# A new issue order for a retention-plus-GELU kernel: one table of 955 words replaced by another

## The chip, the cores and the metric

The kernel runs on one core of one Trainium2 chip. The metric is the time of one execution in microseconds of device time. The engines are named as in the profile: PE (TensorE matmuls), PEld (TensorE weight loads), DVE (VectorE), ACT (ScalarE), POOL (GpSimd) and SP (SyncE, which here only issues DMAs).

## The reference

The first half is a retention layer (a recurrent attention with a decay per head), the second a two-layer network with a tanh GELU. q, k and v are float32 of shape (4, 8, 768, 64), w_in is 512 x 2048, w_out is 2048 x 512, and the result is 3072 x 512.

```python
gamma = 1.0 - 2.0 ** (-5.0 - np.arange(H))
for t in range(S):
    state = gamma * state + einsum('bhd,bhe->bhde', k[:, :, t], v[:, :, t])
    y[:, :, t] = D ** -0.5 * einsum('bhd,bhde->bhe', q[:, :, t], state)
x = y.transpose(0, 2, 1, 3).reshape(B * S, H * D)
h = x @ w_in
g = 0.5 * h * (1 + tanh(sqrt(2 / pi) * (h + 0.044715 * h ** 3)))
out = g @ w_out
```

## The kernel before, in words

**Tiling.** The 768 steps are cut into six chunks c = 0 to 5 of 128 steps. In each chunk and each of the four batches b the retention is three kinds of product: A = k q^T within the chunk, masked by the decay; y = A v plus q times the state carried in; and the state's update. A chunk then gives 512 rows of x, which go through w_in, GELU and w_out. Chunks 0 and 1 do the first layer by plain products (`m1_raw`), chunk 0 the second too (`m2_raw`). Chunks 2 to 5 (first layer) and 1 to 5 (second) use a scheme of seven products on half-size blocks (`m1_w`, `m2_w`), which needs sums of blocks: `xs` from x, `u_w` from w_in, `t_w` from w_out, `s_g` from the GELU's output. All these sums are recorded on one helper line, L447.

**Items and the table.** The work behind the lead-in is recorded as 954 items by `op` and `pe`: each has a number, a kind, the values it needs and gives, and the buffers that it takes and frees. The table `ORDER` names every item once by a letter for the engine (p PE, v DVE, a ACT, g POOL, s SP) and its number. The loop at L1268 emits the items in that order, so the table fixes the order in each engine's queue, the engine of those items that may run on more than one, and which PSUM bank or buffer an item takes (the one that has been free longest, by place in the table). A word like w3 emits three filler matmuls (L193). Each engine works through its queue in order and waits at the first instruction whose inputs aren't there.

**What the numbers stand for** where the prediction names them:

- p168 to p188: retention of chunk 0 (transposes L269, A L291, y L322, state L333). p190 to p236: first layer of chunk 0 (L422), p805 to p826 its second layer (L568). p239 to p274: retention of chunk 1 (transposes L280, A L291, state in L310, y L322, state L333). p276 to p306: first layer of chunk 1. p325 to p360, p451 to p480, p571 to p600, p691 to p716: retention of chunks 2 to 5. p365 to p431, p485 to p551, p605 to p671, p721 to p787: their first layer (L545, 4 matmuls each). p829 to p951: second layer of chunks 1 to 5 (L557, 8 matmuls each).
- L217, L219: copies and casts on ACT, POOL or DVE. L234: scaling by a decay (q, k or v). L342: evA, the masked copy of A out of PSUM. L349: evY, the scaled copy of y to x. L354: evS, four instructions that update the state. L438: GELU. L447: adds out of PSUM (`add`) and all block sums. L704: the transposes of q on DVE (`trq`).
- g0 to g5: POOL's triggers of the last six weight loads (L403, L412); the first two are issued in the lead-in. g6 is the `hold` (L776), a one-element copy that needs the third w_out chunk; all later loads of rows stand behind it.
- s11 to s118: SP's loads of q, k and v, each of 256 KB (L787); q of chunks 3, 4 and 5 comes as one item of 16 DMAs each, s60, s85 and s110 (L730, `loadq`). Stores of results (L578) are in the same queue. The casts of these q blocks are `castq` and `cast2`.

Of the kernel before, what the change touches and what calls it, by code (L numbers as in the profile page):

```python
# [13 lines left out]


ORDER = """
v8 v9 g0 g1 g10 g2 g3 g4 g5 p168 a167 w3 p173 p171 v170 a7 v169 p178 a172 w2 p188 a187 p180
p176 v174 v175 p184 p182 a183 p190 a181 a189 p192 v135 p186 v177 v179 v136 v143 v159 p206
p194 v144 v147 g6 a185 p196 s11 s12 s13 s14 s15 a191 g25 s16 g28 a193 s17 a195 s18 s19 s20
p222 p208 p210 p224 a223 p226 a225 p228 s21 g31 s22 g34 v139 v151 p230 p232 p198 a227 p200  # L20
a209 a205 a197 a229 p212 a231 p234 a221 a211 a199 p236 p202 p214 p216 p805 p218 a201 v146
v160 a233 v23 v163 v164 p204 v138 a213 a215 p806 a207 p220 p807 v155 p808 p809 p810 p811 v24
a203 a219 a217 p812 p813 p814 p817 a815 s35 s36 v26 v152 s37 v162 v140 v27 a818 s38 s39 s40
p239 v237 v238 p245 a244 a235 p820 v243 v141 v156 p242 v240 v241 p248 v247 v246 v29 p261
p823 v142 s41 p824 p825 p264 v263 p266 a265 p826 p276 p278 a827 v148 a275 p280 v158 v32 v33
p257 a277 v30 p251 s42 a279 s43 s44 p282 p284 v154 g54 g55 a821 v165 a249 a255 v256 p260
v250 p254 p262 a281 s45 s46 s47 v258 s816 p286 v253 v252 a283 s822 p288 a287 p268 a267 p272
g48 a49 g51 g52 v259 p270 v166 v269 p274 a57 g58 v273 v149 p290 p292 p294 p296 a291 a293
v271 p298 p300 a289 v137 p302 v307 s60 p304 p325 s61 v150 v308 v310 s62 v157 a295 a297 v311
g312 p343 g53 g56 v309 a285 v145 a299 a301 v50 s63 s819 p337 v323 v324 s64 s65 a335 v342  # L30
a303 g59 p306 v336 v341 a305 p331 g321 a330 g319 g320 a329 v315 p340 v339 v338 g322 p328
v327 p829 p830 v316 a831 p346 v344 g313 p334 g69 v326 v332 v333 p832 v345 p833 p348 p347
p350 p354 p358 v349 p352 p356 v355 p360 p835 p836 v351 p367 a73 a837 v357 v353 p384 p365 v70
g361 g363 a77 a75 p382 v359 a366 a383 v368 g79 v834 s66 s67 s828 s68 p838 p839 p372 p389
p399 p387 v385 a81 g83 g362 g314 v317 p401 p370 a369 g71 s85 s86 s87 g364 a400 a386 v153
v402 a388 a373 p404 a371 v74 v78 g76 a390 p841 p406 p377 v82 p374 v378 a405 a403 a407 a379
p391 g84 v375 a376 v392 v318 a393 p408 v409 p416 a417 s88 p380 a381 p411 a840 s89 g72 s90
g80 p397 a398 p394 v395 a396 p842 v412 a413 v843 v433 v437 v435 v161 p423 a424 p414 p421
p418 v419 v434 a422 g94 p844 p845 a410 a415 g441 v846 s847 g443 g438 g442 p428 p425 v426
g440 a420 v429 p451 a450 p460 a449 v459 s91 a96 a430 p848 v458 s92 p431 a432 p457 v455 v456  # L40
p454 v452 a427 g445 p463 p849 a850 g97 v462 v453 p852 p853 v461 p466 p467 v464 v465 p468
a854 p472 p480 v479 p474 p470 p478 v469 s851 v471 v477 g446 p476 v473 v475 a106 a102 s93 g98
g100 p855 p856 v857 p858 p502 a503 g439 g104 a108 g481 g483 p859 g484 g482 g109 v103 v107
s110 s111 g444 v95 s112 p485 s113 a486 s114 p861 p571 v569 v448 p580 a579 a860 a570 g105
g119 g101 p862 g121 p507 p492 p504 a508 a578 v505 p490 a493 p487 v488 a491 v447 p509 a510
p519 v436 p494 p497 a489 a506 p514 p511 v498 a499 v495 a496 a520 p864 v515 p521 a863 a516
v512 a513 p500 s115 a501 p536 p865 g553 s116 s117 p517 p543 a537 a518 v866 v99 g554 g557
g558 v522 p867 a544 p524 a525 p526 a527 a523 p868 v869 s870 g556 p528 g126 v529 p538 p541
a542 p531 v532 a533 p534 a530 a535 p871 p545 v539 a540 p872 a873 s874 s118 v546 a547 p548
v561 g562 v549 a550 p551 g130 p577 a552 g565 g567 g566 p586 v584 v585 p574 p875 p876 a877  # L50
p878 p879 v575 p583 v573 v572 p588 g563 v576 g560 v581 v582 p587 p590 p592 p598 v589 v591
p596 v595 a127 p594 v593 g601 v555 p600 v599 v564 v559 g603 v880 p881 p882 p884 p605 a883
p885 p639 p622 p607 p624 g604 a123 a606 a623 a125 a886 v597 g131 g133 v625 v608 p612 a626
a613 v120 v128 a640 p887 v132 p888 p610 a609 p617 p641 p644 g602 a611 v618 v642 a645 p627
a628 p614 p629 v615 a619 g122 a630 p648 p656 g568 a657 p631 p620 a616 v889 a621 v632 p646
a647 p634 p637 a638 v124 v635 a636 v673 p658 v674 v659 a633 a660 p890 g134 g677 g678 p691
a643 v649 v689 p661 a662 v690 p891 v892 p663 p651 p665 a129 a664 g680 v652 v666 p654 a650
a655 a653 g681 g682 p700 a699 a698 p697 v695 v696 p668 v669 p671 s893 a672 a667 a670 p898
v675 v687 p894 p895 g685 p694 v693 p703 g686 p706 v705 v692 p899 g679 p901 p902 a900 v903
p904 a896 s897 v701 v702 v704 p905 v684 p707 p708 p714 p710 v709 g683 p716 v715 p712 v711  # L60
v713 g717 g719 p907 p908 a909 a906 p721 p772 p755 p738 p774 v676 a773 a739 a756 p740 p910
a722 v775 p723 a776 p726 v741 v724 g718 g720 p760 g688 p911 a725 a742 a727 p777 p757 p743
v758 a759 p728 a729 a744 p730 a761 v731 a778 v912 p779 a780 p913 p733 v734 a735 a732 p914
v915 p781 v782 a783 p762 a763 p784 v785 p736 p745 p764 a746 v765 p747 s916 v748 a737 v791
v789 v790 p767 p921 p750 g792 v751 a786 a749 v768 p753 p770 p787 a766 a754 a771 a752 v793
a769 a788 v799 p917 p918 a919 s920 p923 p925 a922 a924 v801 v797 p927 v802 v798 v794 g796
g795 v803 p929 p931 p933 p935 a930 v800 v926 v928 p937 a932 a934 a936 v804 v938 p939 v940
p942 p945 p948 p951 s941 v943 v946 s947 a944 a949 a952 s953 a950
"""


# [1239 lines left out]
```

## Time and profile before

| | |
|---|---|
| three runs, us | 208.22, 207.89, 200.37 (median 207.89) |
| the profiled execution, us | 201.67 |
| its span, us | 199.9 |
| mean granted TensorE clock | 0.998 |
| busy PE / PEld / DVE / ACT / POOL, us | 191.1 / 154.8 / 146.1 / 119.0 / 108.9 |
| HBM read and written, MB | 27.64 and 6.29 |

The span runs from the first to the last instruction; the execution's own time is 1.77 us longer. A row of a timeline has its start, its length, the engine, the line of the code, the operation, its tiles and shape, how many instructions are merged, and in brackets how long the engine was idle before it and what ended that. The lengths of matmuls are modelled and overlap the next one, so differences of starts tell PE's pace better than lengths. An arrow like `[0.73 <-DVE st L447]` says that the wait ended with DVE's instruction of line 447 that wrote `st`.

### The profile page before, as it was taken

To read this page: it belongs to the slowest core of one execution; us is meant where nothing else is said; L and a number is where in the kernel's file an instruction comes from. 1 tells how busy PE (TensorE), PEld (TensorE's weight loads), DVE (VectorE), ACT (ScalarE), POOL (GpSimd) and SP (SyncE) were. 2 spreads that over 40 slices of the span, in tenths; PEclk is the share of its full clock that TensorE was granted. 3 is DMA by queue.
4 is the path that set the end of the run, shared out by engine and by line. 5 is a ranking of instruction groups with operands and counts; after the bars stand their busy time and mean duration, and the time that the engine had idled before them with its cause. 6 is when DMAs were issued, how large, how long until landed. Compare 5 with 4: busy or idle time off the path is not lost.

```text
span 199.9 us, 6597 instructions
## 1 busy us (share of the span) xinstructions
PE 191.1 (96%) x2797; PEld 154.8 (77%) x2797; DVE 146.1 (73%) x287; ACT 119.0 (60%) x228; POOL 108.9 (54%) x113
## 2 busy tenths in 40 slices
PE   7899999999999999799998999999999999999993
PEld 2456996456888788688887888888788888888882
DVE  4467013789699997999899685799888776378920
ACT  2476564043757506999734987726799525699411
POOL 0784000042064976790999959998926955602500
PEclk9999999999999999999999999999999999999999
DMA  7999999999899768978997689620002020010204
GB/s 171 288 263 207 207 206 198 256 250 239 202 230 237 112 118 219 272 113 139 226 279 163 98 168 249 217 56 0 3 0 92 19 105 3 0 75 33 107 30 184
DMA packets 95901, 30.16 MB, mean 151 GB/s; under 512 B 88320, under 2 KB 92800, under 8 KB 95872
## 3 DMA queue, kind: packets, MB, share of 16 engines
q1 hardware_dynamic: 85120, 23.45, 50.2%
q0 software_dynamic: 4224, 4.19, 12.7%
q10 hardware_dynamic: 6528, 2.10, 4.2%
q8 instruction: 22, 0.36, 0.7%
q14 instruction: 7, 0.06, 0.1%
HBM read 27.64 MB, written 6.29 MB: 170 GB/s over the span
## 4 chain that ended last, share of the span: by engine, by line
PE 48%; POOL 4%; DVE 2%; issue 1%; ACT 0%; POOLq 0%
PE ps L557 24%; PE ps L545 21%; POOL s_g L447 3%; PE ps L291 1%; PE ps L322 1%; DVE st L354 1%; DVE s_g L447 1%; PE ps L280 1%; DVE o L447 1%; POOL qk L219 1%; PE ps L310 1%; POOL v L234 0%; PE ps L333 0%; ACT o L217 0%; POOLq L447 0%
## 5 line engine op out<-in xcount | busy, mean ns | idle before, releaser
L447 DVE TENSOR_TENSOR st<-ps,st 128x512 f32<-128x512 f32 x48 | 31.6, 683 | 11.9 <-PE ps L545 7.9
L438 ACT ACTIVATE g<-ps 128x512 f16<-128x512 f32 (+1 forms) x56 | 28.2, 540 | 11.1 <-PE ps L422 10.8
L557 PEld LDWEIGHTS <-s_g 128*128 128x128 f16 x320 | 30.9, 98 | 4.7 <-POOL qk L219 0.9
L217 ACT COPY o<-ps 128x512 f32<-128x512 f32 (+1 forms) x28 | 14.4, 526 | 31.9 <-PE ps L557 21.6
L438 ACT ACTIVATE g<-st 128x512 f16<-128x512 f32 x48 | 29.2, 636 | 4.6 <-DVE st L447 4.4
L342 DVE TENSOR_TENSOR a<-ps,mask 128x512 f16<-128x512 f32 x44 | 27.4, 682 | 5.1 <-PE ps L291 5.1
L422 PE MATMUL ps<-x,w_in 128*128 128x256 f16 (+1 forms) x320 | 29.8, 251 | 0.4 <-DMA w_in<-in_moe_w_in_dram 0.4
L217 ACT COPY st<-ps 128x512 f32<-128x512 f32 x48 | 26.4, 595 | 4.6 <-PE ps L545 4.3
L422 PEld LDWEIGHTS <-w_in 128*128 128x128 f16 x320 | 25.6, 98 | 3.7 <-DMA w_in<-in_moe_w_in_dram 0.5
L545 PEld LDWEIGHTS <-w_in 128*128 128x128 f16 x256 | 25.0, 98 | 3.7 <-issue 0.6
L557 PEld LDWEIGHTS <-g 128*128 128x128 f16 x240 | 22.9, 98 | 3.2
L447 POOL TENSOR_TENSOR s_g<-g 128x512 f16<-128x512 f16 x18 | 21.2, 1188 | 5.3 <-ACT g L438 5.3
L545 PEld LDWEIGHTS <-u_w 128*128 128x128 f16 x192 | 18.5, 98 | 4.5 <-issue 1.6
L447 POOL TENSOR_TENSOR s_g<-g,s_g 128x512 f16<-128x512 f16 x11 | 13.2, 1202 | 13.2 <-PE ps L545 9.6
L557 PE MATMUL ps<-t_w,s_g 128*128 128x256 f16 x160 | 19.5, 273 | 0.6 <-POOL qk L219 0.6
L557 PE MATMUL ps<-w_out,s_g 128*128 128x256 f16 x160 | 19.9, 273 | 0.0
L545 PE MATMUL ps<-xs,u_w 128*128 128x256 f16 x128 | 18.2, 273 | 1.7 <-DVE st L447 1.2
L557 PE MATMUL ps<-w_out,g 128*128 128x256 f16 x160 | 19.0, 273 | 0.0
L545 PE MATMUL ps<-xs,w_in 128*128 128x256 f16 x128 | 18.1, 273 | 0.0
L545 PE MATMUL ps<-x,w_in 128*128 128x256 f16 x128 | 17.6, 272 | 0.0
L234 POOL TENSOR_TENSOR v<-ld,cst 128x512 f16<-128x512 f32 x15 | 16.6, 1120 | 0.0
L447 DVE TENSOR_TENSOR o<-ps,o 128x512 f32<-128x512 f32 (+1 forms) x18 | 10.7, 597 | 8.0 <-ACT o L217 4.6
(71 smaller groups left out, 284.8 us busy)
## 6 DMA issues: line engine op xcount, KB each, us to landing
ld<-in_v_dram SPq DMA_DIRECT2D x19, 256.0 KB, 4.4
ld<-in_k_dram SPq DMA_DIRECT2D x17, 256.0 KB, 4.4
out_dram<-o SPq DMA_DIRECT2D x8, 512.0 KB, 3.9
ldq<-in_q_dram SPq DMA_DIRECT2D x48, 64.0 KB, 2.8
w_in<-in_moe_w_in_dram POOLq DMA_DIRECT2D x4, 512.0 KB, 10.7
w_out<-in_moe_w_out_dram POOLq DMA_DIRECT2D x4, 512.0 KB, 15.9
ld<-in_q_dram SPq DMA_DIRECT2D x5, 256.0 KB, 5.4
out_dram<-o SPq DMA_DIRECT2D x5, 256.0 KB, 3.4
```

The lines of the kernel that those rows point to most:

```text
L217: eng.copy(out=out, in_=in_)
L219: eng.tensor_copy(out=out, in_=in_)
L234: eng.tensor_tensor(out=o, in0=heads(src, sw), in1=heads(cst[:, col:col + H].unsqueeze(2), sw).broadcast_to([128, NHP, 2, Dh]), op=ALU.mult,)
L280: nc.tensor.transpose(out=ps[m][j * 64:(j + 1) * 64, n + i, hp], in_=h16[nm, c, b][rows, 2 * hp + j], identity=iden[rows, rows],)
L291: nc.tensor.matmul(out=ps[j][m * 64:(m + 1) * 64, hp], lhsT=t[j * 64:(j + 1) * 64, 1, hp, m * 64:(m + 1) * 64], rhs=t[j * 64:(j + 1) * 64, ...
L310: nc.tensor.matmul(out=ps[b][j * 64:(j + 1) * 64, hp], lhsT=st_of(b)[sl, hp], rhs=qkT[c, b][sl, 0, hp], start=(hp == 0), stop=False, skip_ ...
L342: eng.tensor_tensor(out=a_sb[c, b, j], in0=ps, in1=mask[:, j], op=ALU.mult)
L422: nc.tensor.matmul(out=out, lhsT=w_in_sb[wi][:, kc, wr * 128:(wr + 1) * 128], rhs=xT[c][:, kc, t0:t1], start=(kc == 0), stop=(kc == NHP - ...
L438: nc.scalar.activation(out=out, in_=in_, func=AF.Gelu_apprx_tanh, scale=1.0)
L447: eng.tensor_tensor(out=out, in0=in0, in1=in1, op=op)
L545: nc.tensor.matmul(out=ps[:, f], lhsT=m1_lhs(lk, kc, 2 * g + f), rhs=x[:, kc], start=(n in FIRST and kc == 0 and f == 0), stop=(n in (1, 5 ...
L557: nc.tensor.matmul(out=ps, lhsT=m2_lhs(c, lk, fp, a), rhs=m2_rhs(rk, fp), start=(first and fp == 0), stop=(n in (1, 5, 6) and fp == NP - 1 ...
```

## The change

Only the table `ORDER` is replaced, and nothing else. The new one was generated with later landing times assumed for the loads of rows and of the q blocks. It has the same 954 items; the filler w2 is left out and w3 stays. The loads of q, k and v keep their order among themselves; stores change places among them. 320 PE items change places among each other, and some items change engine: POOL has 42 of the s_g sums of kind `sumg` where it had 38 (DVE 22 for 26), 13 scalings for 15 (DVE 3 for 1), 17 casts for 18 and 2 `castq` for 3 (ACT one more of each). One `evS1` goes from DVE to ACT and one `evY1` from ACT to DVE. The first lines of the diff, and those that hold the places of which the prediction speaks:

```diff
--- before.py
+++ after.py
 ORDER = """
-v8 v9 g0 g1 g10 g2 g3 g4 g5 p168 a167 w3 p173 p171 v170 a7 v169 p178 a172 w2 p188 a187 p180
-p176 v174 v175 p184 p182 a183 p190 a181 a189 p192 v135 p186 v177 v179 v136 v143 v159 p206
-p194 v144 v147 g6 a185 p196 s11 s12 s13 s14 s15 a191 g25 s16 g28 a193 s17 a195 s18 s19 s20
-p222 p208 p210 p224 a223 p226 a225 p228 s21 g31 s22 g34 v139 v151 p230 p232 p198 a227 p200
...
-g440 a420 v429 p451 a450 p460 a449 v459 s91 a96 a430 p848 v458 s92 p431 a432 p457 v455 v456
-p454 v452 a427 g445 p463 p849 a850 g97 v462 v453 p852 p853 v461 p466 p467 v464 v465 p468
-a854 p472 p480 v479 p474 p470 p478 v469 s851 v471 v477 g446 p476 v473 v475 a106 a102 s93 g98
...
+v8 v9 p168 a167 p180 w3 p173 a172 v179 p171 v169 g10 v170 g0 p176 a7 g1 g2 g3 v174 v135 g4
+g5 p188 a187 p178 v175 p182 a181 p190 v136 p192 v139 v143 v159 v160 a189 v138 p186 p206 p208
+a185 p210 a207 a205 p212 v147 p194 a193 p196 v163 v162 v151 p198 p214 a209 a197 a195 a211
+a191 a213 g6 s11 v23 s12 p222 p224 a221 v152 p226 p200 v24 a199 p228 a227 p230 a229 s13 s14
+p805 s15 s16 s17 p216 s18 g25 v26 s19 v154 s20 g28 v155 s21 g31 s22 g34 s35 s36 a225 p202
...
+s88 s89 s90 p421 a422 p451 v450 a396 g437 g438 p460 v459 v458 g442 g435 p428 p425 a420 a449
+v429 v426 a427 p848 p463 v461 p457 v456 v462 p454 v453 a430 v455 p849 a850 s851 p852 v452
+p853 v439 p431 a432 g445 g446 p466 p468 v465 v464 p467 p470 a98 a100 p480 s91 p474 p472 v469
+v471 v434 p478 p476 v475 v447 v473 a102 v103 a854 g448 g94 p855 g96 g481 g483 p856 p858 g482
...
+p904 p905 a906 p907 p908 v695 p910 v692 p706 a909 v705 p708 p707 v704 p911 p710 v709 v912
+p714 p712 v711 v713 p716 v715 p913 p914 v915 s916 g717 g719 p757 p755 g718 a756 p721 v758
+a722 p772 a773 p738 g720 a739 p723 v724 a759 p762 a763 p774 a725 v775 p726 a727 p740 p743
```

More of the change, by code (lines that the diff above doesn't have):

```diff
@@ L16 @@
 ORDER = """
-v8 v9 g0 g1 g10 g2 g3 g4 g5 p168 a167 w3 p173 p171 v170 a7 v169 p178 a172 w2 p188 a187 p180
-p176 v174 v175 p184 p182 a183 p190 a181 a189 p192 v135 p186 v177 v179 v136 v143 v159 p206
-p194 v144 v147 g6 a185 p196 s11 s12 s13 s14 s15 a191 g25 s16 g28 a193 s17 a195 s18 s19 s20
-p222 p208 p210 p224 a223 p226 a225 p228 s21 g31 s22 g34 v139 v151 p230 p232 p198 a227 p200
-a209 a205 a197 a229 p212 a231 p234 a221 a211 a199 p236 p202 p214 p216 p805 p218 a201 v146
-v160 a233 v23 v163 v164 p204 v138 a213 a215 p806 a207 p220 p807 v155 p808 p809 p810 p811 v24
@@ L23 @@
[L23 to L39, printed above, removed]
-g440 a420 v429 p451 a450 p460 a449 v459 s91 a96 a430 p848 v458 s92 p431 a432 p457 v455 v456
@@ L41 @@
-p454 v452 a427 g445 p463 p849 a850 g97 v462 v453 p852 p853 v461 p466 p467 v464 v465 p468
-a854 p472 p480 v479 p474 p470 p478 v469 s851 v471 v477 g446 p476 v473 v475 a106 a102 s93 g98
[L43 to L68, printed above, removed]
+v8 v9 p168 a167 p180 w3 p173 a172 v179 p171 v169 g10 v170 g0 p176 a7 g1 g2 g3 v174 v135 g4
+g5 p188 a187 p178 v175 p182 a181 p190 v136 p192 v139 v143 v159 v160 a189 v138 p186 p206 p208
@@ new lines @@
+a185 p210 a207 a205 p212 v147 p194 a193 p196 v163 v162 v151 p198 p214 a209 a197 a195 a211
+a191 a213 g6 s11 v23 s12 p222 p224 a221 v152 p226 p200 v24 a199 p228 a227 p230 a229 s13 s14
+p805 s15 s16 s17 p216 s18 g25 v26 s19 v154 s20 g28 v155 s21 g31 s22 g34 s35 s36 a225 p202
+a201 p232 a215 p806 s37 p234 a223 a233 v27 v164 s38 s39 p204 a203 p218 a217 v156 p807 a177
+p236 v148 v149 p808 p220 a219 s40 p809 p810 p811 v157 p812 p813 p814 p817 a231 p239 a237
+p245 a243 v238 a815 a235 v144 a818 v244 p820 a821 p823 v29 v30 p248 g54 g55 v246 v247 s41
@@ new lines @@
+s42 s43 p242 s44 p824 v241 v240 p825 p261 p251 a249 p266 p264 v263 p184 v32 v33 v158 s45 s46
+a265 s47 s822 p826 s816 a183 a827 p276 a275 p278 p280 p282 p284 a277 a279 v166 v146 v250
+v140 v141 v165 a281 p257 v255 a256 p254 v253 v252 p286 p260 v258 p262 v259 p288 p268 a283
+v267 p272 p270 v269 v142 a285 a48 g51 g49 a52 a287 p274 v273 g57 p290 p292 a289 p294 p296
+a291 p298 v271 p300 p302 p304 a293 s60 a58 p343 v307 g308 g53 s61 s62 a295 a297 v311 v309
+v312 v50 p337 s63 s64 g56 s65 s828 g59 a299 s819 s66 a301 v315 p325 a303 p306 v335 v341 a323
@@ new lines @@
+a324 v336 a342 v150 a305 g319 g320 v313 v137 p829 p340 v338 v339 p331 a330 p346 a329 v344
+v345 g316 g318 p830 a831 p328 v327 v326 p334 v332 v333 g314 g317 p832 p833 p347 p348 p354
+g81 p350 v349 v353 p360 p356 v355 p358 p352 v351 g361 v834 a77 g363 p835 p836 v357 p838 a73
+a837 v78 v359 p401 p839 g79 v82 p399 a400 v402 p382 s67 a383 p365 a366 a69 g71 p367 p372
+a403 a373 v153 p404 a405 s68 s85 p370 a371 v321 p384 g362 p387 g75 g364 a388 v145 p841 p377
+s86 v368 v385 v378 p406 a369 a386 g322 v70 g310 a379 v74 a407 p389 a390 p374 v375 a376 p408
@@ new lines @@
+p391 v392 g83 v409 p842 p411 v412 a840 v843 p380 p397 p414 a381 v433 p844 g84 g72 g76 p845
+s87 p416 a398 a415 v80 a393 a410 v161 a413 p423 g441 v846 s847 a417 p394 p418 v395 v419 a424
+s88 s89 s90 p421 a422 p451 v450 a396 g437 g438 p460 v459 v458 g442 g435 p428 p425 a420 a449
+v429 v426 a427 p848 p463 v461 p457 v456 v462 p454 v453 a430 v455 p849 a850 s851 p852 v452
+p853 v439 p431 a432 g445 g446 p466 p468 v465 v464 p467 p470 a98 a100 p480 s91 p474 p472 v469
+v471 v434 p478 p476 v475 v447 v473 a102 v103 a854 g448 g94 p855 g96 g481 g483 p856 p858 g482
@@ new lines @@
+a104 a106 p485 a486 s92 p487 s93 v479 s110 s111 g443 g101 v857 p502 v477 g97 v488 g444 v95
+p859 p861 a503 a108 a860 p862 a863 s112 g105 s113 p507 s114 a508 p490 g484 a491 p571 v570
+v569 g440 p580 v579 a578 p511 p509 a510 p504 v505 v99 p492 p494 a489 p536 a493 p514 v495
+a496 a537 p497 p519 v498 v512 p864 p865 a506 a520 a513 v515 p543 a499 g109 v436 p500 p517
+a501 a516 p541 g553 a518 v866 v559 g119 s115 g555 g557 a544 a542 p524 p521 p538 v539 p526
+a527 a525 v522 g121 g554 p548 p545 p867 a523 v546 p531 v532 a540 a547 p528 v529 p868 v869
@@ new lines @@
+p871 g558 a533 p534 a530 s870 s116 s117 a535 v549 a550 v107 g561 g562 p872 a873 p583 v581
+p574 p586 p551 v585 v582 a552 p875 p876 p878 v573 g565 p577 g566 p587 v572 v584 p588 p594
+p590 v575 v576 p596 v589 a877 g126 p598 p592 g122 v591 a127 v595 v593 g601 g131 g603 p600
+g602 p879 v880 g604 p605 a123 p607 a606 v608 a129 p639 p641 p881 p622 a640 v642 a623 p629
+a630 s118 s874 g567 v120 v597 a609 g563 p646 p882 g568 p644 v599 p627 a647 a628 p624 v124
+v625 a883 a626 a643 p651 p634 v635 p631 p610 v632 a611 p612 a613 p656 a645 a633 v652 v128
@@ new lines @@
+p884 a636 p885 p614 v615 a616 p648 v649 p658 g560 p617 a886 p620 p637 v618 p654 a650 g564
+p887 a619 a638 p663 a657 a621 g673 a664 p888 v556 v134 p890 p661 v659 a660 v889 a655 a662
+p668 v669 a653 a670 g681 p891 v892 p894 p665 v666 g682 a667 v679 s893 p898 p895 v674 v684
+g125 a133 p671 g683 a672 g687 g676 a896 s897 v677 v678 g130 g680 v685 p899 p700 v698 v699
+a900 v675 p691 a689 a690 v686 g688 p901 p902 v903 p703 v132 v702 v701 p697 p694 v696 v693
+p904 p905 a906 p907 p908 v695 p910 v692 p706 a909 v705 p708 p707 v704 p911 p710 v709 v912
@@ new lines @@
+p714 p712 v711 v713 p716 v715 p913 p914 v915 s916 g717 g719 p757 p755 g718 a756 p721 v758
+a722 p772 a773 p738 g720 a739 p723 v724 a759 p762 a763 p774 a725 v775 p726 a727 p740 p743
+v741 a742 p777 p728 a729 p760 a761 p730 v731 p745 p767 v768 a776 a746 p733 v734 p917 p764
+v765 p779 a732 a744 p747 a769 a735 a780 v748 p736 a778 p750 v751 p784 a737 p781 v789 v782
+a766 v785 v790 p753 p770 a752 p921 a749 a771 a786 v797 a754 v793 v794 p787 a788 a783 v801
+v802 p918 a919 s920 p923 p925 p927 v798 a922 g804 a924 p929 a930 p931 g800 v799 v791 v795
@@ L69 @@
+a932 g796 p933 a934 p935 v928 v803 a936 v926 v792 p937 v938 p939 v940 s941 p942 p945 p948
+p951 a949 v943 a944 v946 s947 a952 s953 a950
 """
```

## The prediction

> **What bounds the kernel now.** I read the page's engine table first, then the stages, then TensorE's timeline, then the queues that TensorE stands behind.
>
> ```profile
> span 199.9 us, 6597 instructions
> PE 191.1 (96%) x2797; PEld 154.8 (77%) x2797; DVE 146.1 (73%) x287; ACT 119.0 (60%) x228; POOL 108.9 (54%) x113
> 20.00:60.00 40.00, 39.99 (x603) 29.44 (x604) 23.82 (x56) 18.61 (x42) 7.50 (x11) 1.00 1.09 223
> 60.00:100.00 40.00, 38.35 (x682) 32.45 (x680) 37.48 (x70) 28.12 (x53) 28.43 (x29) 1.00 0.86 180
> 100.00:140.00 40.00, 39.35 (x635) 34.24 (x633) 33.42 (x64) 25.12 (x47) 36.54 (x37) 1.00 0.66 154
> ```
>
> The columns after the length are busy PE, PEld, DVE, ACT, POOL, then the granted clock, DMA share and GB/s. From 20 us on PE is short of work in a few places only; DVE is busy 37.5 of 40 us in the third row, so a PE wait there is mostly a wait for its queue. The places themselves:
>
> ```profile
> 20.01 10.35 PE L422 MATMUL ps<-x,w_in 128*128 128x256 f16 x144 [0.35 <-DMA w_in<-in_moe_w_in_dram]
> 66.20 0.77 PE L280 MATMUL ps<-iden,qk 64*64 64x64 f16 x32
> 67.19 0.64 PE L291 MATMUL ps<-qkT 64*64 64x128 f16 x32 [0.22 <-DVE qkT L219]
> 80.71 0.60 PE L545 MATMUL ps<-xs,u_w 128*128 128x256 f16 x4 [0.73 <-DVE st L447]
> 85.02 0.60 PE L545 MATMUL ps<-xs,u_w 128*128 128x256 f16 x4 [0.49 <-DVE st L447]
> 105.77 0.83 PE L557 MATMUL ps<-t_w,s_g 128*128 128x256 f16 x6 [0.64 <-POOL qk L219]
> 140.60 0.61 PE L545 MATMUL ps<-xs,u_w 128*128 128x256 f16 x4 [0.44 <-DVE st L354]
> ```
>
> The idle figures understate each loss, because a matmul's modelled end runs past the start of the next. I use starts instead: a block of L545 (4 matmuls) advances PE by 0.44, one of L557 (8) by 0.87, 32 transposes by 0.32 where nothing waits. Then 65.09 to 67.19 cost 2.10 for 0.88 + 0.32, so 0.90 is lost; before 80.71 and 81.31 it is 0.89 + 0.16; before 85.02, 0.66; around 105.77 (104.74 to 106.43 for one L557 block) 0.81; before 140.60 0.76. Sum of losses: 4.18 us. At the end there is only the drain after PE's last product.
>
> What stands behind them:
>
> ```profile
> 76.52 0.61 POOL L219 CAST qk<-ldq 128x512 f16<-128x512 f32 x1 [2.74 <-DMA ld<-in_k_dram]
> 77.16 0.71 DVE L704 STREAM_TRANSPOSE qkT<-qk 128x512 f16<-128x512 f16 x1 [0.26 <-POOL qk L219]
> 94.95 0.61 POOL L219 CAST qk<-ldq 128x512 f16<-128x512 f32 x1 [4.81 <-DMA ldq<-in_q_dram]
> 95.52 2.28 POOL L447 TENSOR_TENSOR s_g<-g 128x512 f16<-128x512 f16 x2
> ```
>
> Twice POOL's queue stands at the cast of a q block that hasn't landed. The second time 4.81 us pass and the s_g sums queue behind it; PE's block at 104.74 waits for those.
>
> **What the change does, part by part.** All 320 PE items, the loads and their order stay; the words of the table change places, and some items change engine. One filler, the word w2 (two L193 matmuls), goes. All gains and losses are therefore in the waits and in the lead-in.
>
> *Lead-in.* PE stands at 20.01 for w_in's second chunk whatever is before it. In the table after, one L422 block more (p208, 0.45 by the starts 22.21 to 22.66) is ahead of that gate, and one mm_s of chunk 0 (p184, 0.25) is put behind. So 0.20 less PE work follows the gate. The cost: p176 now stands directly behind p171 and needs the second of ACT's 1.0 us qkT copies (13.18 and 14.61 in the trace; from about 14.55 to 15.6 now). PE idles about 0.9 there; that idle replaces fillers and a wait, and PE still reaches the gate near 19.7. The cover left is 0.3. Value: -0.20, between -0.45 and +0.3.
>
> *First w_out chunk.* p805 (m2 of chunk 0) comes 12 blocks after the gate: 4 of 0.88 and 8 of 0.45 make 7.1, so PE asks at 27.1. The w_out loads issue at 14.41 at the earliest and land 13.2 us later at the shortest (least of the tile's issue-to-landing times): 27.6. PE waits about 0.5. Between 0.3 and 0.8.
>
> *POOL's cast g10 ahead of the triggers.* The words g10 g0 g1 replace g0 g1 g10. That cast waits for v of (0,3) until 13.85, so w_in's third trigger moves from 11.39 to 14.46 and the others follow; POOL's hold and SP's rows hang on the third w_out chunk. I take 0: the chunks land one after another about 2.5 apart (PE and DVE are released at 20.0, 25.5, 30.1, POOL's hold at 32.7), and the shortest issue-to-landing of w_in, 7.6, would still put the third chunk at 22.1, when PE asks at 22.7. Upper end +3.0, as a rival below.
>
> *First row block.* DVE does the scales v29 and v30 and three evA before the evA (v240) that yi p264 wants: after T1's copies near 42.8 that is five steps of 0.60 (evA and scale starts) and 0.68 for itself, 46.5 to 47.1; PE arrives at 47.1. Value +0.2, between 0 and 0.5.
>
> *The five losses.* (a) 0.90: between T2 and A of c=2 there are now an L422 and an L557 block (1.75) where only one L422 block and a T2 were, and the 1.53 us scale v50 is ahead of the copies. Gone. (b) 1.05: evS v359 and the add v402 free the banks that p372 and p384 want. DVE still stands at the q block (v78 now), so v359 ends near 78.9 and v402 near 80.2; PE asks at 80.7 and 82.2. Gone, with 1.8 to spare. (c) 0.66: DVE's order is too different to follow; half, 0.33. (d) 0.81: eight s_g words now precede g94, the cast of the second q block. p431's gelu is done near 100, then g445 and g446 at 1.12 each end at 102.3, and PE asks near 104.7. Gone. (e) 0.76: evS v597 still stands behind two adds and a transpose, but p612, which wants its bank, comes 2 us later; half, 0.38. Sum -3.5, between 0 and -4.2.
>
> *A new bank wait.* p757 p755 p721 p772 p738: the last takes the bank of p757, which add v758 frees, and that add waits for the snap of p755. From the end of p755 PE has two blocks (0.87); the snap (0.59) and the add (0.68) with both hand-overs need 1.5. Loss 0.65, between 0.3 and 0.9.
>
> *Waits that I don't see.* The other 300 places are as densely packed as before, where the old table left 4.2 of loss. New places: between 0 and 4.2. The queue causes that I can name (a cast ahead of its landing, a long scale ahead of copies) are rarer, so I take a third, 1.4.
>
> *The engines' sums.* Four s_g sums go from DVE (0.42) to POOL (1.16), two scales from POOL (1.04) to DVE (0.69), two casts from POOL (0.61) to ACT. POOL gains about 1.3 us, DVE loses 0.3. No PE time by itself.
>
> Sum: -0.20 + 0.5 + 0 + 0.2 - 3.5 + 0.65 + 1.4 = -0.95. The profiled execution took 201.67 (span 199.9, 1.77 around it): **200.7 us**. The median shown, 207.89, belongs to runs at 207.89 and 208.22; the third is 200.37. The sum stands beside the profile's and the low one; no view says why two are 3.8% longer.
>
> **The rivals.**
>
> *R1, the triggers land as late as they are issued.* If issue-to-landing is a fixed time, the third w_in chunk comes 3.0 later, 25.5, where PE asks at 22.7 (+2.8), w_out's first chunk at 30.6 (+0.2 beyond the 0.5 counted), and the hold and every row shift by 3. Sum 203.7, with the unseen losses at their upper end 206.5. For it: POOL's queue is in order. Against: equal spacing of the landings under unequal issue gaps. It decides once the third chunk lands after 22.7. This is the case on the slow side.
>
> *R2, DVE stands at the first q block.* v78 and v82 now both stand ahead of the bank-freeing evS and add, and POOL's cast2 ahead of the xs sums. The spare is 1.8 (p372 at 80.7 against v359 at 78.9); each us of landing beyond 78.3 is one of PE. Landing 5 later, it adds 3.1: 203.8, and 205.6 with half of (c) to (e) lost. For it: the 10.5 us of SP issues that the block needs; against: SP's order up to it is nearly the same.
>
> *R3, POOL and DVE collide.* DVE's 0.42 us sums took up to 1.38 while POOL summed. If POOL's four more sums each meet one and PE pays 0.95, it is +3.8: 204.5. [...]
>
> *R4, the long runs are runs of late rows.* If at 207.89 the rows land several us later, the old table pays it in POOL's queue (94.95), and the new one, with eight sums ahead of that cast, doesn't. Then the median falls to about 201.5, faster by 3%. For it: DMA share near or over 1 until 50 us and three casts that wait for landings; against: two runs within 0.2% of each other look like a level, not like lateness.
>
> *R5, the level stays.* The runs again fall mostly on the upper one: 200.7 x 208.0 / 200.4 = 208.3, no change to the median.
>
> **How the numbers follow.** Chances: forecast 0.56, R1 0.08, R2 0.06, R3 0.05, R4 0.13, R5 0.12. The forecast's own range is 198.5 to 203.5: 197.8 would need all losses gone and none new. The range reaches up for R1 to R3 and R5, 198.0 to 208.4. About 2% is what can be told from no change here, 4 us. Faster: R4 and a sliver of the forecast, 0.16. Slower: the upper ends of R1 to R3 (0.12) and 0.03 of R5. Same: 0.69.
>
> **What would show it.** Right: PE's row before 67, 80 and 105 without a wait, POOL's cast of the second q block behind the sums and not waiting, a wait of about 0.5 for w_out near 27, one of 0.65 before p738 near 172, the span at 197.5 to 200. Wrong: a PE wait of over 2 us at 22.7 (R1), PE's wait at 80 back and larger (R2), DVE sums of 1.38 in larger number in 60 to 110 (R3), or losses of over 4 us in places not named here.

## The result: 3.3% slower, and the profile after

| | before | after |
|---|---|---|
| median of six runs, us | 201.30 | 207.66 |
| ratio, 95% interval | | 1.033 (1.026 to 1.040) |
| profiled execution / its span, us | 201.67 / 199.9 | 207.54 / 205.8 |
| granted clock of the profiled execution | 0.998 | 0.983 |

The ratios leave out runs more than 1.5% above the fastest of their kernel, here before's two near 208 and after's one at 212.38; of such runs the traces of e5 (211.61) and e8 (207.47) show TensorE waiting 4.1 and 4.7 us near 17 us for a late load of v, and half clock with it (16 L422 matmuls took 2.78 in e8 for a usual 1.92).

The head of the page of the kernel after, its line of the granted clock in 40 slices, and the stages (columns as in the prediction):

```profile
span 205.8 us, 6591 instructions
PE 193.6 (94%) x2795; PEld 156.6 (76%) x2795; DVE 154.8 (75%) x285; ACT 120.2 (58%) x230; POOL 109.5 (53%) x113
PEclk9999999999999969999999999999999969999999
60.00:100.00 40.00, 36.78 (x618) 31.01 (x615) 35.84 (x64) 25.21 (x47) 27.59 (x27) 0.96 0.80 171
100.00:140.00 40.00, 40.00 (x684) 35.22 (x683) 35.73 (x64) 28.63 (x52) 36.10 (x36) 1.00 0.71 162
140.00:180.00 40.00, 37.95 (x490) 32.50 (x489) 32.12 (x54) 21.62 (x42) 24.08 (x22) 0.96 0.11 41
```

and of the kernel before the line of the clock and the last of these stages:

```profile
PEclk9999999999999999999999999999999999999999
140.00:180.00 40.00, 39.56 (x521) 34.56 (x520) 29.43 (x52) 27.92 (x54) 22.56 (x21) 1.00 0.10 38
```

The same 320 PE items take 2.5 us more busy time, and DVE, with two instructions fewer, 8.7 us more: work became slower, not more. On DVE what reads PSUM kept its length: the 48 adds out of PSUM take 31.6 us in both pages, the 44 evA 27.4 and 27.3. What grew are the sums of blocks in SBUF, the s_g ones alone from 21.0 to 27.1. The clock line has two dents, in the first and the third stage shown, and these are the stages in which PE is short of work; from 100 to 140 it never waits. TensorE's timeline at the two places, and at w_out's first chunk:

```profile
27.92 1.04 PE L568 MATMUL ps<-w_out,g 128*128 128x512 f16 x4 [0.41 <-DMA w_out<-in_moe_w_out_dram]
68.51 0.42 PE L291 MATMUL ps<-qkT 64*64 64x128 f16 x16 [0.81 <-DVE qkT L219]
70.36 0.24 PE L291 MATMUL ps<-qkT 64*64 64x128 f16 x1
72.78 0.41 PE L291 MATMUL ps<-qkT 64*64 64x128 f16 x15 [2.18 <-DVE a L342]
73.38 0.64 PE L291 MATMUL ps<-qkT 64*64 64x128 f16 x16 [0.18 <-DVE a L342]
73.95 3.28 PE L557 MATMUL ps<-w_out,g 128*128 128x256 f16 x16
164.11 1.19 PE L291 MATMUL ps<-qkT 64*64 64x128 f16 x48 [1.96 <-DVE qkT L219]
165.23 5.33 PE L557 MATMUL ps<-t_w,s_g 128*128 128x256 f16 x32
```

*Place 1* is chunk 2's A (p340 and p328): 0.81 for the copies of qkT, then 2.18 inside p328, whose second bank is freed by an evA. *Place 2* is p703, chunk 5's A: 1.96 for the copies v698 and v699. Behind each wait stands a slow stretch: 16 L557 matmuls took 1.92 elsewhere and 3.28 here, 32 of them 5.33 where e6 below has 3.67. By starts, as in the prediction, places 1 and 2 lose about 5.7 and 4.3 us with their slow stretches. Counted so over all of PE's rows after 18 us, the losses grew by 5.4 to 6.2 us, depending on what is taken as the undisturbed pace of a row; the span grew by 5.9.

What VectorE and POOL did ahead of p703, in the kernel after:

```profile
158.58 1.37 DVE L447 TENSOR_TENSOR s_g<-g,s_g 128x512 f16<-128x512 f16 x1
159.87 1.37 DVE L447 TENSOR_TENSOR s_g<-g 128x512 f16<-128x512 f16 x1
161.28 1.25 DVE L447 TENSOR_TENSOR s_g<-s_g,g 128x512 f16<-128x512 f16 x1
162.46 1.26 DVE L447 TENSOR_TENSOR s_g<-g 128x512 f16<-128x512 f16 x1
163.64 0.74 DVE L219 COPY qkT<-ps 128x512 f16<-128x512 f16 x2
158.34 2.62 POOL L447 TENSOR_TENSOR s_g<-g 128x512 f16<-128x512 f16 x2
160.93 1.33 POOL L447 TENSOR_TENSOR s_g<-g,s_g 128x512 f16<-128x512 f16 x1
162.22 1.22 POOL L234 TENSOR_TENSOR v<-ld,cst 128x512 f16<-128x512 f32 x1
```

and in the kernel before, around the same products:

```profile
156.38 0.41 DVE L447 TENSOR_TENSOR s_g<-g 128x512 f16<-128x512 f16 x1
158.52 1.89 DVE L342 TENSOR_TENSOR a<-ps,mask 128x512 f16<-128x512 f32 x3 [0.43 <-PE ps L291]
156.38 1.42 POOL L447 TENSOR_TENSOR s_g<-s_g,g 128x512 f16<-128x512 f16 x1
157.76 1.33 POOL L447 TENSOR_TENSOR s_g<-g 128x512 f16<-128x512 f16 x1
```

Read starts and ends together. After: each of the four DVE sums from 158.58 on begins while a POOL instruction runs and ends about 0.3 behind that one's end (160.96 and 161.24, 162.26 and 162.53). Before: the two sums of 156.38 start together, DVE's takes its usual 0.41 and POOL's comes out at 1.42 for a usual 1.16. Both would fit two engines of which one stands while the other works; that is an inference from these rows. The copies out of PSUM (0.74 for two, and 0.76 in e6 with POOL standing) keep their length, and so do the evA (1.89 for three): six from 166.50 on take 3.64, nearly all of it with POOL idle, and six in e6 take 3.64 with POOL at work. The old table ran evA on DVE while POOL summed; the new one set six DVE sums, with the copies behind them, against a row of POOL's sums. Place 1 reads alike: v150, v313 and v137 take 1.17, 1.37 and 1.37 ahead of the evA, from 68.38 to 72.1, while POOL sums from 68.11 to 75.4. Here the collision is read from the rows; no run took POOL's sums away at place 1.

### The profile page after: what moved, and what is told of

Its sections match the earlier page's. It is cut to its first block, busy times and chain, and to the rows that moved or that the text cites. A ratio compares the mean times of both kernels' runs of the same rounds, so it can differ in the third digit from the quotient of the medians.

```text
span 205.8 us, 6591 instructions
## 1 busy us (share of the span) xinstructions
PE 193.6 (94%) x2795; PEld 156.6 (76%) x2795; DVE 154.8 (75%) x285; ACT 120.2 (58%) x230; POOL 109.5 (53%) x113
## 4 chain that ended last, share of the span: by engine, by line
PE 76%; DMA 9%; DVE 8%; SPq 3%; POOL 1%; issue 1%; ACT 0%
PE ps L557 29%; PE ps L545 24%; PE ps L422 7%; PE ps L568 7%; DVE s_g L447 6%; DMA w_out<-in_moe_w_out_dram 6%; DMA ld<-in_v_dram 3%; SPq L164 3%; PE ps L322 3%; PE ps L291 3%; PE ps L280 1%; PE ps L310 1%; PE ps L333 1%; DVE qkT L219 1%; POOL w_in L403 1%
## 5 line engine op out<-in xcount | busy, mean ns | idle before, releaser
L447 DVE TENSOR_TENSOR st<-ps,st 128x512 f32<-128x512 f32 x48 | 31.6, 683 | 10.5 <-PE ps L545 5.4
L557 PEld LDWEIGHTS <-s_g 128*128 128x128 f16 x320 | 31.8, 101 | 4.9 <-DVE s_g L447 0.2
L342 DVE TENSOR_TENSOR a<-ps,mask 128x512 f16<-128x512 f32 x44 | 27.3, 678 | 4.0 <-PE ps L291 4.0
L422 PE MATMUL ps<-x,w_in 128*128 128x256 f16 (+1 forms) x320 | 30.0, 251 | 0.0
L422 PEld LDWEIGHTS <-w_in 128*128 128x128 f16 x320 | 25.8, 98 | 3.7 <-DVE x L219 0.2
L447 POOL TENSOR_TENSOR s_g<-g 128x512 f16<-128x512 f16 x18 | 21.1, 1177 | 12.6 <-ACT g L438 12.6
L545 PEld LDWEIGHTS <-w_in 128*128 128x128 f16 x256 | 24.9, 98 | 3.0
L557 PEld LDWEIGHTS <-g 128*128 128x128 f16 x240 | 23.7, 101 | 3.8 <-issue 0.2
L447 POOL TENSOR_TENSOR s_g<-g,s_g 128x512 f16<-128x512 f16 x16 | 19.3, 1224 | 12.4 <-DVE s_g L447 12.2
L557 PE MATMUL ps<-w_out,g 128*128 128x256 f16 x160 | 20.8, 285 | 0.0
L545 PEld LDWEIGHTS <-u_w 128*128 128x128 f16 x192 | 18.7, 98 | 2.6 <-issue 0.4
L557 PE MATMUL ps<-t_w,s_g 128*128 128x256 f16 x160 | 20.6, 288 | 0.0
L447 DVE TENSOR_TENSOR s_g<-g 128x512 f16<-128x512 f16 x22 | 18.0, 830 | 3.1 <-ACT g L438 3.1
L557 PE MATMUL ps<-w_out,s_g 128*128 128x256 f16 x160 | 19.7, 273 | 0.0
L447 POOL TENSOR_TENSOR xs<-x 128x512 f16<-128x512 f16 x8 | 9.3, 1157 | 16.0 <-DVE x L349 16.0
L545 PE MATMUL ps<-xs,u_w 128*128 128x256 f16 x128 | 17.6, 272 | 0.0
L545 PE MATMUL ps<-xs,w_in 128*128 128x256 f16 x128 | 17.4, 273 | 0.0
L545 PE MATMUL ps<-x,w_in 128*128 128x256 f16 x128 | 16.9, 273 | 0.0
```

Of the source, the lines that this page charges most:

```text
L342: eng.tensor_tensor(out=a_sb[c, b, j], in0=ps, in1=mask[:, j], op=ALU.mult)
L422: nc.tensor.matmul(out=out, lhsT=w_in_sb[wi][:, kc, wr * 128:(wr + 1) * 128], rhs=xT[c][:, kc, t0:t1], start=(kc == 0), stop=(kc == NHP - ...
L447: eng.tensor_tensor(out=out, in0=in0, in1=in1, op=op)
L545: nc.tensor.matmul(out=ps[:, f], lhsT=m1_lhs(lk, kc, 2 * g + f), rhs=x[:, kc], start=(n in FIRST and kc == 0 and f == 0), stop=(n in (1, 5 ...
L557: nc.tensor.matmul(out=ps, lhsT=m2_lhs(c, lk, fp, a), rhs=m2_rhs(rk, fp), start=(first and fp == 0), stop=(n in (1, 5, 6) and fp == NP - 1 ...
```

## The experiments

All times are medians; ratios are to the kernel before, run beside it on the same chip. In e1 to e5 the table takes two lines less, so L445 there is L447 here, L289 L291, L543 L545.

**e1: the copies ahead of the sums (place 2)**

```diff
-... a896 s897 v677 v678 g130 g680 v685 p899 p700 v698 v699 a900 ...
+... a896 s897 p899 p700 v698 v699 v677 v678 g130 g680 v685 a900 ...
```

> Theory (queue and collisions): in the changed kernel p703 waits 1.96 us before 164.1 because DVE has six s_g sums ahead of the two copies of kT (v698, v699), and the sums take 0.69 to 1.37 each while POOL sums too. Here the two copies, with p899 and p700 that they follow, stand ahead of v677, v678, v685. DVE would start them near 160.5, PE wouldn't wait at p703, and the half clock of 3.4 us that follows the wait (1.7 us lost) would be gone as well: 205.8 - 2.4 - 1.7 = about 201.7 of span, 203.4 of time. The first long wait, near 70 to 73, stays with its half clock. Rival (the wait is the data's: the k rows or the casts of chunk 5 come late): the copies still start near 163.6 and the span stays within 0.5 of 205.8.

206.13 us, ratio 1.019 (1.011 to 1.028), where 203.4 was expected. The wait at p703 went, and 1.70 us of it came back at the next reader, p904's second half, which waits for the sums themselves; all but one (0.52) of the last five ahead of it were as slow as before (1.25 to 1.37). No half clock followed that wait (clock 1.00 from 166.64 to 170.05). So moving the copies moves the wait and doesn't remove it; that points to the sums' length, which e6 tests.

**e3: e1, and at place 1 three sums behind the evA**

```diff
-... a342 v150 a305 g319 g320 v313 v137 p829 ... v332 v333 g314 ...
+... a342 a305 g319 g320 p829 ... v332 v333 v150 v313 v137 g314 ...
```

> Both places mended by order alone: the copies first as above, and near 70 the sums v150, v313, v137 go behind the eight evA of chunk 2 (v338 to v333), so that the banks that p334 wants come free near 70. Theory: both waits and both stretches of half clock are gone: 205.8 - 4.1 - 1.5 (first place) - 2.4 - 1.7 (second) = about 196.1, and perhaps 0.5 to 1 comes back elsewhere: span 196 to 197.5, time 198 to 199, 1% faster than the kernel before. Rival (the new table is slower all over, and another queue takes the place of each wait removed): span 200 to 204.

204.11 us, ratio 1.012 (1.004 to 1.020), in the rival's range and not at the 198 to 199 of the theory. The 2.18 us wait and its half clock went (16 L555 matmuls at 71.43 take 1.92), and most of the wait came back in pieces (TensorE's timeline of e3):

```profile
69.00 0.42 PE L289 MATMUL ps<-qkT 64*64 64x128 f16 x16 [0.81 <-DVE qkT L217]
79.23 0.60 PE L543 MATMUL ps<-x,w_in 128*128 128x256 f16 x4 [0.76 <-DVE x L347]
86.91 1.20 PE L543 MATMUL ps<-xs,u_w 128*128 128x256 f16 x8 [0.76 <-DVE st L445]
163.67 3.01 PE L555 MATMUL ps<-t_w,s_g 128*128 128x256 f16 x26 [1.70 <-DVE s_g L445]
```

The one run of e1 at clock 1.0 took 204.26, as long as e3: this single run suggests that what e3 gained over e1 is about the half clock.

**e4: fillers in the waits, first try**

```diff
-... p334 ... p703 ...
+... w9 p334 ... w8 p703 ...
```

> The table of the changed kernel with fillers in the two long waits: w9 (nine 128x512 matmuls on zeros, 0.21 to 0.25 us each) ahead of p334 and w8 ahead of p703. Nothing else moves; the waits for DVE stay. Theory (the clock falls to half for 3.4 us because PE stood idle for about 2 us): no half clock at 73.4 and 165.6, each worth 1.7 us: span about 202.4, time about 204.2. Rival (the half clock has another cause, or fillers on zeros don't count): two stretches of half clock remain, span 205.8 or up to 0.5 more, because fillers run past the end of the wait.

207.81 us, ratio 1.029 (1.021 to 1.037). At place 2 the fillers did what they should: p703 waited 0.23, and no half clock followed (32 L555 matmuls in 3.67 us). At place 1 they were in the wrong spot: the wait lies inside p328, so nine fillers ran behind it, at half clock (3.53 us, where nine take 2.11 in e7):

```profile
73.69 3.53 PE L191 MATMUL spin_ps<-zero 128*128 128x512 f16 x9
```

What one place gained, the other lost. Two of the four runs show hardly any half clock (0.999) and still took 207.42 and 207.69: the fillers' own time is the likely loss there, but no trace of such a run was kept.

**e5: POOL's sums later, a test that tested nothing**

```diff
-... p671 g683 a672 g687 g676 a896 s897 v677 v678 g130 g680 v685 p899 p700 v698 v699 a900 ...
+... p671 a672 a896 s897 v677 v678 v685 p899 p700 v698 v699 g683 g687 g676 g130 g680 a900 ...
```

> DVE's order stays that of the changed kernel, all six sums ahead of the copies; POOL's g683 g687 g676 g130 g680 come behind them in the table, so that POOL has nothing to sum from about 158.5 until the copies are through. Theory (collision): DVE's sums from 158.5 on fall from 1.25 to 1.37 us each to about 0.42, the copies start near 160.5, no wait at p703, span about 201.7, time 203.4, as with the copies moved. Rival (DVE simply has too much ahead of the copies, whatever POOL does): sums unchanged, wait of 2 us and span of 205.8 stay; a little longer if POOL's sums are then late for p904 to p913.

207.79 us, ratio 1.027 (1.018 to 1.036), level with the changed kernel, and it had to be: POOL's own order is unchanged, and a word's place among other engines' words makes no engine wait. p703 waited 1.96 again, and the four VectorE sums took 1.25 to 1.37. Nothing follows for the collision.

**e6: POOL's sums behind an instruction that waits for VectorE**

```diff
-... p671 g683 a672 g687 g676 a896 s897 v677 v678 g130 g680 v685 ... v686 g688 p901 ...
+... p671 a672 a896 s897 v677 v678 v685 ... v686 g688 g683 g687 g676 g130 g680 p901 ...
```

> The changed kernel with five of POOL's instructions (sums g683 g687 g676 g680 and the cast g130) behind POOL's g688. g688 waits for v686, the last of VectorE's sums at this place, so POOL stands still while VectorE sums from 158 to 163 us. Theory (a VectorE sum of two SBUF rows runs three times as long while POOL sums too: 1.25 to 1.37 us beside POOL in the changed kernel's rows, 0.42 alone): the four sums there take about 0.42 us each, the copies of qkT end some 3 us earlier, the wait of 1.96 us ahead of p703 is gone and with it the half clock of 3.41 us after it; place 1 keeps its 2.2 us. Span about 202 to 203, time 203.5 to 204.5. Rival (the sums are slow by themselves or through something else, transfers for one): they stay at 1.25 to 1.37 us, the wait at p703 stays near 2 us, time 207 to 208.

203.27 us, ratio 1.002 (0.998 to 1.007), a little below the 203.5 to 204.5 expected. VectorE's, POOL's and TensorE's timelines of e6 (this execution took 205.55: from 20 us on everything stands 2 us later, after a wait of 1.06 for w_in and a half-clock stretch, 16 L422 matmuls in 3.52):

```profile
160.61 0.41 DVE L447 TENSOR_TENSOR s_g<-g,s_g 128x512 f16<-128x512 f16 x1
160.95 0.41 DVE L447 TENSOR_TENSOR s_g<-g 128x512 f16<-128x512 f16 x1
161.39 0.42 DVE L447 TENSOR_TENSOR s_g<-s_g,g 128x512 f16<-128x512 f16 x1
161.73 0.42 DVE L447 TENSOR_TENSOR s_g<-g 128x512 f16<-128x512 f16 x1
162.09 0.76 DVE L219 COPY qkT<-ps 128x512 f16<-128x512 f16 x2
159.60 0.81 POOL L219 CAST qk<-ld 128x512 f16<-128x512 f32 x1
163.66 1.16 POOL L447 TENSOR_TENSOR s_g<-g,s_g 128x512 f16<-128x512 f16 x1 [3.25 <-DVE s_g L447]
164.11 0.86 PE L291 MATMUL ps<-qkT 64*64 64x128 f16 x48
164.91 3.67 PE L557 MATMUL ps<-t_w,s_g 128*128 128x256 f16 x32
```

The same four VectorE sums, on the same data, take 0.41 to 0.42 with POOL standing. From the first of them to the copies it is 1.48 us instead of 5.06. p703 doesn't wait, and the 32 L557 matmuls behind it take 3.67 instead of 5.33. One edit of POOL's queue gives back 4.4 of the 6.4 us by the medians, 3.1 of the 3.3 points by the ratios. This shows the collision to be the cause at place 2.

Place 1 was left as it was, and whether its wait is followed by half clock differs from run to run of this one kernel: three runs at clock 1.0 took 201.74 to 202.26, five at 0.992 took 203.06 to 203.43, and the other two, at 0.981 and 0.975, took 205.55 (the one shown, with its half clock near 18 us besides) and 209.25. The means of the three and the five are 1.36 apart, an estimate of the price of one half-clock stretch here.

**e7: fillers where the waits are**

```diff
-... p328 ... p703 ...
+... w9 p328 ... w8 p703 ...
```

> The changed kernel with nine idle matmuls on zeros ahead of p328 and eight ahead of p703, so that TensorE works through most of its two long waits; VectorE and POOL are as late as before. Theory (a wait of about 2 us costs itself and, one stretch of the clock later, 3.41 us at half clock): the waits shrink to about 0.3 us each, the real work after them starts as late as in the changed kernel, no stretch at half clock is left, and the span falls by the 1.5 to 1.75 us of each: about 202.5, time 204 to 204.5. Rival (the half clock costs nothing, since TensorE would wait for VectorE in those stretches anyway): time 207 to 208.

205.27 us, ratio 1.015 (1.008 to 1.023). TensorE's timeline:

```profile
70.11 2.11 PE L193 MATMUL spin_ps<-zero 128*128 128x512 f16 x9
72.27 0.77 PE L291 MATMUL ps<-qkT 64*64 64x128 f16 x16
73.58 1.92 PE L557 MATMUL ps<-w_out,g 128*128 128x256 f16 x16
163.30 1.19 PE L291 MATMUL ps<-qkT 64*64 64x128 f16 x48 [0.23 <-DVE qkT L219]
```

The lateness of VectorE is all still there (the L557 block starts at 73.58 for 73.95), but the clock is 1.00 in the three stages from 60 to 180 and the block takes 1.92 for 3.28. Useless matmuls left the kernel faster than the changed one, by 2.4 us by the medians and by 1.8 points (3.6 us) by the ratios: 1.2 to 1.8 for each half-clock stretch, with the 1.36 of e6 between them. The time was a little above the 204 to 204.5 expected.

**e8: e3 and e6 together**

> The earlier run with both places moved (copies of qkT ahead of the sums; v150 v313 v137 behind v333; 204.1 us there), and POOL's five instructions behind g688 as well. Theory: the 1.70 us that TensorE still waited at 164 for the sums goes, no half clock, span about 200.7, time 202 to 202.7, the same as the kernel before within 1%. Rival (the wait only moves on to POOL's sums that are now late, p910 or p913): time 204 again.

201.37 us, ratio 0.998 (0.995 to 1.002), below the 202 to 202.7 expected. The 1.70 us of e1 and e3 at 164 is gone and nothing came in its place there. With the two places mended the new table is level with the old one.

**e9 and e10: a version that beats both**

```diff
 e9, from e8:
-... a297 v311 v309 v312 ... g316 g318 p830 ... v333 v150 v313 v137 g314 g317 ... g81 p350 ...
+... a297 v150 v137 v311 v312 ... g316 p830 ... v333 v313 v309 g317 ... g81 g318 g314 p350 ...
 e10, from e9:
-... v137 v311 v312 v50 ... v333 v313 v309 ...
+... v137 v311 v50 ... v333 v312 v313 v309 ...
```

> The run above (e8) and four more moves around 62 to 77 us: v150 and v137 into VectorE's idle time ahead of v311, v309 behind v313, POOL's g318 and g314 behind its cast g81. Theory: of the waits that the run with both places moved still had, 0.97 us ahead of p340 (copies of qkT) and 0.92 ahead of p401 (x) shrink by 0.5 to 0.9 us each: span about 199.3, time 200.5 to 201.5, level with the kernel before or up to 1% faster. Rival (each wait taken away here comes back at the next thing VectorE is late with, as at 87 us): time 202 to 202.7, as e8.

> The fastest kernel so far (e9, 199.8 us) with one more word moved: VectorE's sum v312, which takes 1.15 us beside POOL's casts of v rows, from ahead of the copies of qkT at 67 to behind v333. Theory (p340 waits 0.94 us at 68 because the copies stand behind that sum): the wait falls to 0.2 or less, and the work behind v333 has room for a sum of 0.4 to 1.3 us; span about 197.2, time 198.5 to 199.5, over 1% faster than the kernel before. Rival (the sum only moves the lateness to x, which p401 waits for): a wait of 0.5 to 1 us at 77 to 79 and the time of e9 again, 199.8 to 200.5.

e9: 199.77 us, ratio 0.989 (0.980 to 0.998). The waits at 79 and 87 of e3 went; the one ahead of p340 stayed, though the sum taken away there was 1.2 long. e10: 199.50 us, ratio 0.991 (0.987 to 0.994), so 1% faster than the kernel before and, by the two ratios, 4% faster than the one after; from e9 to e10 nothing measurable was gained. VectorE's row and two of TensorE's in e10 tell why:

```profile
65.87 1.26 DVE L447 TENSOR_TENSOR s_g<-g 128x512 f16<-128x512 f16 x1
68.18 0.42 PE L291 MATMUL ps<-qkT 64*64 64x128 f16 x16 [0.43 <-DVE qkT L219]
81.61 1.03 PE L545 MATMUL ps<-xs,u_w 128*128 128x256 f16 x8 [0.64 <-POOL xs L447]
```

The sum at 65.87 is v315, which took 0.41 in e9, where it ran behind POOL's scalings of v (L234). Moved forward by the removal of v312, it met them and took 1.26. Of 1.15 us removed, 0.3 reached TensorE (a wait of 0.43 for 0.77), and the wait for POOL's sum xs at 81.61 took it back: 0.64, where e9 waited 0.33.

## Why the prediction was wrong

**The term that failed is "waits that I don't see", 1.4 us.** The prediction gave the new table a third of the old one's loss for places that it didn't follow. It measured 9.0: of the 10.0 at places 1 and 2, 0.97 is loss (a), which was counted elsewhere. The reason given, that the queue causes that could be named are rarer in the new table, counted two causes and not the third. The collision was a rival (R3) at a chance of 0.05 and with a price of 3.8 for the four sums more that POOL got. Its cause was the right one (VectorE's sums take 0.41 to 0.42 with POOL standing and 1.25 to 1.37 beside its sums, e6 against the kernel after) and its measure wrong: not how many sums POOL has mattered, but how many DVE sums stand beside a row of POOL's with a wanted copy or evA behind them; e6 leaves the number of sums as it was and gains 4.4 us. VectorE's 39 s_g sums took 21.0 us before (10.9, 6.6 and 3.5 in three groups); its 35 in the changed kernel 27.1 (18.0, 5.9, 3.2). At 0.41 each, the excess is 5.0 and 12.8. Both queues' order was in the table, so this could have been read before the run. The paragraph on the engines' sums has the same error: it took 0.42 for every DVE sum, forecast 0.3 us less work for DVE, and DVE had 8.7 more.

The rows show the collision on both sides: VectorE's 0.41 becomes 1.25 to 1.37, POOL's 1.16 becomes 1.42 where the two start together (156.38 in the kernel before), and copies and evA, which read PSUM, keep their lengths (0.74 and 0.76 for two, 3.64 and 3.64 for six). Why the two engines slow each other in these sums no trace shows.

**No term had the half clock.** Before's page shows no dent, so nothing made the prediction ask what a wait of 2 us costs beyond itself. In the kernel after, the two stretches at half clock are 3.41 us long each, and their starts (73.42 and 165.58) are 92.16 apart, 27 such lengths. Counted on from there the trace falls into a grid of 3.41 us, which stands elsewhere in another run (a boundary at 162.17 here, at 163.22 in e1). Stretches of that grid, in the kernel after (four rows) and in e1 (last row), columns as in the stages:

```profile
70.01:73.42 3.41, 1.05 (x24) 0.52 (x26) 3.41 (x5) 0.94 (x2) 3.33 (x4) 0.99 0.62 97
73.42:76.84 3.42, 3.42 (x30) 2.45 (x30) 3.42 (x6) 0.00 (x0) 3.17 (x4) 0.51 1.03 228
162.17:165.58 3.41, 1.39 (x51) 1.11 (x52) 3.41 (x7) 0.00 (x0) 2.65 (x4) 0.99 0.02 5
165.58:169.00 3.42, 3.42 (x19) 2.44 (x17) 3.42 (x7) 0.37 (x1) 1.07 (x1) 0.51 0.00 0
163.22:166.64 3.42, 1.72 (x33) 1.24 (x22) 3.42 (x5) 0.00 (x0) 2.66 (x3) 1.00 0.02 5
```

PE busy 1.05 and 1.39 of a stretch: the next runs at half clock. Busy 1.72: it doesn't. On the grids of the kernels before and after, from 5 us on, half clock follows these two and a last one of the kernel before (195.87 to 199.28, busy 0.65); every other stretch has PE busy 2.60 or more, and none of them is followed by it. In e5 p703 waited the same 1.96, and no half clock followed (ten L555 matmuls behind it took 1.27, where 16 undisturbed take 1.92). Counted on from e5's half clock near 80 (16 L555 matmuls in 3.32 at 79.40), the grid split that wait, with PE busy an estimated 2.0 of the stretch in which it ended. So by these rows the clock drops when PE is busy less than some value between 1.39 and 1.72 of a stretch, and with the 1.36 of e6 a wait of 2 us costs an estimated 3.3 when it falls inside one stretch, 2 when the grid splits it. Waits of 1.96 and 2.18 us were enough here.

Point by point, the prediction's other steps:

- *Lead-in, triggers:* right in this execution. Between 18 and 60 us PE has one wait, the 0.41 at 27.92; w_in's last two chunks, asked for 3.3 later, landed at 22.73 and 25.27, for 22.46 and 25.46 before. R1 is out. The lead-in gained about nothing, inside its range: at 57 us, with the same work done, PE is 0.71 later, of which 0.57 is the wait for w_out.
- *First w_out chunk:* forecast 0.5, measured 0.41 (0.57 by starts). The number is partly luck: the step took the old issue at 14.41 and 13.2 to the landing, where the triggers' own paragraph moves that issue back; it was issued at 16.23 and landed 11.64 later.
- *First row block:* forecast 0.2, measured below 0.15.
- *The five losses, -3.5:* (b) to (e) went, but for 0.37 left at 88 to 89. (a) did not go, it became 0.97: the copies of chunk 2 wait behind three sums at 62.96 to 66.5 that POOL's scalings of v stretch (2.38 for two, then 1.26). The step followed the order in the queue and took the usual lengths. Sum -2.8.
- *Bank wait ahead of p738:* forecast 0.65, measured none.
- *R2:* DVE never stood at the first q block. (Its 205.6 doesn't follow from its terms: half of the losses (c) to (e) is 1.1, which makes 204.9.) *R4, R5:* the runs near 208 of the kernel before are not a level of the kernel (201.3, 202.0, 202.4 and 201.9 in four comparisons), so neither says anything of the change. R4's late rows do occur, as a late load of v near 17 us in the traces of e5 and e8, which have the new order; no trace shows the cause of before's 208.

Sum by the measured terms: 0.57 - 2.8 + 9.0 = 6.8, for a span that grew by 5.9; the 0.9 between them is spread over small differences that were not followed. By the medians of the runs the account is shorter: place 2 with its half clock 4.4 (e6; 4.3 by starts), place 1's half clock 1.4 (runs of e6), together 5.8 of 6.4. The wait itself at place 1 is about what the vanished old losses had paid for: e6 at clock 1.0 took 201.9, where the kernel before took 202.4. That place 1's wait has the collision as its cause is argued from the rows alone.

## What to carry to other kernels

Where two engines slow each other, as here a VectorE sum takes 0.41 us alone and 1.25 to 1.37 beside POOL's, an instruction's length is not a constant of the queue's plan: price a VectorE sum by what POOL does at that moment, and look where a wanted copy stands behind several of them. The cure that gave most here (4.4 us, e6) was order within POOL's own queue, with the engine that nobody waits for held behind an instruction that needs the other one. Ask of each wait of about 2 us or more what the clock does after it (waits of 1.96 and 2.18 were followed by half clock here); fillers are worth trying where the wait can't be removed (2.4 us in e7).

## What the runs showed of the hardware

- A VectorE sum of two SBUF operands of 128x512 f16 took 0.41 to 0.42 us alone and 1.25 to 1.37 beside POOL's sums or its scalings of rows (0.69 and 0.82 at 157.21 and 157.83 in the kernel after, where it met only the last 0.4 and 0.5 us of a POOL instruction); shown by e6 on the same four instructions for the sums, by e9 and e10 on v315 for the scalings.
- TensorE's clock fell to half for 3.41 us after stretches of 3.41 us in which it was busy 1.05 and 1.39 us (the kernel after), and didn't after one with 1.72 (e1); one such stretch at half clock cost about 1.36 us by runs of one kernel (e6), 1.2 to 1.8 by e7. The same kernel has it in some runs and not in others (e6: three at clock 1.0, five at 0.992).
- Fillers in both waits kept the clock at 1.00 from 60 to 180 us and made the changed kernel 2.4 us faster (e7); with the nine of place 1 behind the wait instead, they took 3.53 us and the kernel stayed at the changed one's time (e4).
